# Cosine attention and a GELU layer on one core: score passes split by heads and laid beside the values passes

## The chip, the core and the metric

The kernel runs on one core of one Trainium2 chip. The metric is the time of one execution in microseconds (us). Before the change three runs took 401.39, 401.69 and 401.60 us, a median of 401.6 us. The engines are named as in the profile: PE (TensorE matmuls), PEld (its weight loads), DVE (VectorE), ACT (ScalarE), POOL (GpSimd), SP (SyncE, which issues most DMAs).

## What is computed

```python
q, k, v: (8 batches, 12 heads, 448 rows, 64)          # float32, as is everything below
q_n = q / (norm(q) + 1e-6);  k_n = k / (norm(k) + 1e-6)
p   = softmax(q_n @ k_n.T / tau)                       # tau = 0.1
x   = (p @ v), heads side by side: (3584, 768)
out = gelu(x @ moe_w_in) @ moe_w_out                   # 768 -> 2048 -> 768
```

## The kernel before, in words

**Units of work.** The 12 heads of a batch are three groups of four heads (`NQ = 3`, 24 groups in all). A group's rows are cut into `C = 7` chunks of 64 keys. The order of every instruction is written out by hand, and each engine executes its own list strictly in the order in which the code issues to it.

**A score pass** is `scores` (L232-244) for one chunk: four 64x64 matmuls that cover the four quarters of the array, two with rows 0-63 and two with rows 64-127. It fills a pair of PSUM banks, and one ACT instruction (`exps`, L252) turns the pair into `pt` in bf16. There are three such pairs, numbered 0, 1 and 2; `visit(1, 2)` (L647) makes the next two score passes into pairs 1 and 2.

**A values pass** is one chunk of `values` (L317): again four 64x64 matmuls, two with the array's rows 0-63 and two with rows 64-127, that accumulate `o` over the seven chunks in a pair of banks. `weighted` (L371) makes the seven passes and lets DVE multiply `o` by the inverse sums into `x` (`normalise`, L362).

**Stages.** For batch b the program runs `attention(b)` and then `first(b)`. `first(b)` is the layer 768 -> 2048 (`hp`, L462, 96 matmuls of 448 columns, GELU on ACT, L887). The second layer (`op`, L399, 384 columns) of the batch before is cut into single matmuls in the list `fill`, and `attention(b)` spends them between stretches of attention with `run()`: the tuple `parts` says how many each `run()` takes. There are 96 of them in the odd batches and 128 in the even ones. I number them from 1. A piece is 16 of them, accumulated in one PSUM bank and copied out by DVE (L403). Two banks, called mm0 and mm1 in `mm_tile` (L102), serve the pieces alternately, so piece n can start only when DVE has copied piece n-2. The `hp` blocks of `first` use the same two banks besides the three pairs; the table `pairs` in `first` says which block of two goes to which pair.

**Sums of the softmax.** From batch 2 on the sums are not made by PE. POOL adds up the seven chunks of one group during `attention(b)` and of another during `first(b)` (`folded`, L263); DVE adds up the third itself in `first(b)` (`gathered`, L265-270, seven instructions). DVE then turns each total into inverse sums in `turned_all` (L276, L278, L281) and `inverted_all` (L290, L294), and lays them out in `spread` (L357). `turned_all` starts with two transposes (`ta`, L276) that read what POOL has added up.

**Norms.** For later groups ACT squares (L158), DVE reduces (L168), ACT makes a logarithm and an exponential (L175, L180), DVE the inverse (`se` L186, `rn` L188), and POOL scales q and k (`scale`, L204). The scaled q and k are transposed by DMA.

**Before, attention from batch 3 on** visits seven stretches, with a `run()` ahead of each: visits 1, 2, seven values passes, visit 1; visits 2, 1, 0; visits 2, 0, values, visit 2; three times visits 0, 2, 1; visits 1, 2, values, visit 1. That is 21 score passes and 21 values passes a batch. Score passes run ahead: those of batch b's stage belong to the third group of batch b and the first two of batch b+1. In batch 7 only seven are left, and visits beyond them do nothing.

Of the kernel before, what the change touches and what calls it, by code (L numbers as in the profile page):

```python
# [10 lines left out]
BF16 = mybir.dt.bfloat16  # L11
# [5 lines left out]
def kernel(  # L17
# [280 lines left out]
    def sums(g, chunks=range(C)):  # L298
        for c in chunks:
            if c == 0:  # L300
                bank_t[g, "sm"] = ps_acc.tile([128, 512], F32, tag="sm", name=f"sm{g}") if g < NQ else \
                    mm_tile(f"sm{g}", aside=0)
            for s in range(2):
                if g < NQ:
                    nc.tensor.matmul(bank_t[g, "sm"][64 * s:64 * (s + 1), :S],  # L305
                                     lhsT=ones2.rearrange("p a h r -> p (a h r)"), rhs=pt_t[g, s, c],
                                     start=(c == 0), stop=(c == C - 1), tile_position=(0, 64 * s))
                    continue

                half = 2  # L310
                for i in range(2) if c == half else ((c - (c > half)) % 2,):
                    r = 32 * (2 * s + i)
                    cols = slice(i * S // 2, (i + 1) * S // 2) if c == half else slice(0, S)
                    nc.tensor.matmul(bank_t[g, "sm"][r:r + 32, cols], lhsT=ones, rhs=pt_t[g, s, c][:, cols],  # L314
                                     start=(c < 2), stop=(c >= C - 2), tile_position=(0, r))

    def values(g, chunks=range(C), p=None):  # L317
        for c in chunks:
# [328 lines left out]
    def visit(*pairs):  # L647
        for p in pairs:
            g, c = divmod(at[0], C)
            at[0] += 1  # L650
            if g < NG:
                scores(g, ((0, c), (1, c)), p)
                exps(g, ((0, c), (1, c)))

    def attention(b, fill):
        fill = list(fill)
        if b == 1:
            parts = iter((20, 13, 14, 17, 16, 16))
        elif b == 2:
            parts = iter((22, 12, 12, 13, 11, 13, 11, 11, 11, 6, 6))  # L660
        elif len(fill) == 128:
            parts = iter((20, 18, 18, 18, 18, 18, 9, 9))
        else:
            parts = iter((14, 13, 14, 14, 14, 13, 7, 7))

        def run(n=None):
            for _ in range(next(parts) if n is None else n):
                fill.pop(0)()

        def norms(n):  # L670
            if n < len(groups):
                logs(n)
                roots(n)
                done[root] = n + 1

        def inverted_norms(n):
            if n < len(groups):
                inverses(n)

        def squared(n, i):  # L680
            if n < NU:
                square(n, ((nc.scalar, i),))
                done[square] = n + 1

        def reduced(n, i):
            if n < NU:
                reduce(n, i)
                done[reduce] = n + 1

        x_t[b] = xp.tile([128, KD, S], BF16, tag="x", name=f"x{b}")  # L690
        g0, u = b * NQ, b * NQ + 1
        run()
        if b == 1:
            upto(scale, u + 3)
            upto(load_v, b + 2)
            upto(transposes, u + 3)
            upto(load_qk, g0 + NQ + 2)
            upto(square, u + 4)
            visit(0, 1, 2)
            run()  # L700
            visit(0, 1, 2)
            run()
            upto(load_qk, g0 + NQ + 3)
            visit(0, 1)
            upto(square, u + 5)
            run()
            visit(0, 1, 2)
            both(g0, 0)
            upto(load_v, b + 3)
            upto(load_qk, g0 + NQ + 4)  # L710
            visit(1, 2)
            upto(reduce, u + 4)
            run()
            visit(1, 2, 0)
            both(g0 + 1, 1)
            visit(2, 0)
            logs(6)
            roots(6)
            run()
            both(g0 + 2, 2)  # L720
            inverses(6)
            done[root] = 7
        elif b == 2:
            upto(scale, u + 3)
            upto(load_qk, g0 + 6)
            upto(transposes, u + 3)
            upto(scale, u + 4)
            upto(load_qk, g0 + 7)
            upto(transposes, u + 4)
            visit(0, 1, 2)  # L730
            run()
            visit(0, 1, 2)
            norms(9)
            inverted_norms(9)
            upto(scale, u + 5)
            upto(transposes, u + 5)
            upto(load_qk, g0 + 9)
            upto(square, u + 6)
            run()
            visit(1, 2)  # L740
            total(g0)
            weighted(g0, 0)
            visit(1, 2)
            squared(u + 6, 0)
            run()
            visit(1, 2, 0)
            run()
            reduced(u + 5, 0)
            visit(1, 2)
            squared(u + 6, 1)  # L750
            total(g0 + 1)
            weighted(g0 + 1, 0)
            visit(1, 2)
            reduced(u + 5, 1)
            folded(g0 + 2, range(C - 1))
            run()
            for i in range(2):
                reduced(u + 6, i)
            visit(1, 2, 0)
            folded(g0 + 2, range(C - 1, C))  # L760
            upto(load_v, b + 3)
            run()
            visit(1, 2, 0)
            run()
            visit(1, 2, 0)
            run()
            visit(1, 2, 0)
            norms(10)
            run()
            turned_all(g0 + 2)  # L770
            run()
            inverted_norms(10)
            inverted_all(g0 + 2)
            visit(1, 2)
            weighted(g0 + 2, 0)
            visit(1)
        else:
            upto(scale, u + 5)
            upto(transposes, u + 5)
            upto(load_qk, g0 + 9)  # L780
            visit(1, 2)
            weighted(g0, 0)
            visit(1)
            reduced(u + 5, 0)
            squared(u + 6, 0)
            folded(g0 + 2, range(3))
            run()
            reduced(u + 5, 1)
            visit(2, 1, 0)
            folded(g0 + 2, range(3, 6))  # L790
            run()
            reduced(u + 6, 0)
            for h in range(2):
                spread(g0 + 1, h)
            visit(2, 0)
            weighted(g0 + 1, 1)
            visit(2)
            squared(u + 6, 1)
            folded(g0 + 2, range(6, 7))
            upto(load_v, b + 3)  # L800
            run()
            visit(0, 2, 1)
            run()
            reduced(u + 6, 1)
            visit(0, 2, 1)
            norms(2 * b + 6)
            turned_all(g0 + 2)
            run()
            inverted_norms(2 * b + 6)
            inverted_all(g0 + 2)  # L810
            visit(0, 2, 1)
            run()
            run()
            for h in range(2):
                spread(g0 + 2, h)
            visit(1, 2)
            weighted(g0 + 2, 0)
            visit(1)
        assert not fill, len(fill)

    def first(b):
# [3 lines left out]
        nc.scalar.preload_act_table_set(GELU_SET)  # L825
        u = (b + 1) * NQ + 1
        hps = dict(early) if b == 0 else {}
        pairs = ({0: 1, 2: 0, 6: 1, 8: 0}, {2: 0, 4: 1, 6: 2, 8: 0}, {2: 2, 4: 1, 8: 2})[min(b, 2)]
        ahead = 6 if b else 5

        def mm(m, kds):
# [12 lines left out]
        if b == 0:  # L844
            upto(square, u + 3)
            upto(scale, u + 1)
            upto(transposes, u + 1)
            upto(load_wo, 4)
            upto(reduce, u + 3)
        elif b == 1:  # L850
            upto(scale, u + 1)
            upto(transposes, u + 1)
            upto(load_qk, (b + 1) * NQ + 5)
            upto(square, u + 3)
            upto(reduce, u + 2)
        elif b + 1 < B:
            for n in range(3, 5):
                upto(scale, u + n)
                upto(transposes, u + n)
                upto(load_qk, (b + 1) * NQ + 4 + n)  # L860
            folded((b + 1) * NQ + 1)
            if u + 4 < NU:
                square(u + 4, ((nc.scalar, 0), (nc.scalar, 1)))
            if u + 5 < NU:
                square(u + 5, ((nc.scalar, 0),))
            upto(reduce, u + 5)
            gathered((b + 1) * NQ, 0)
            turned_all((b + 1) * NQ)
            inverted_all((b + 1) * NQ)
            spread((b + 1) * NQ, 0)  # L870
            spread((b + 1) * NQ, 1)
            turned_all((b + 1) * NQ + 1)
            inverted_all((b + 1) * NQ + 1)
            done[square] = u + 6
# [94 lines left out]
```

## Time and profile before

| what | value |
|---|---|
| median of three runs | 401.6 us |
| the profiled execution's own time | 401.45 us |
| its span, first to last instruction | 399.6 us |
| PE busy | 393.0 us (98%) |
| ACT, DVE, POOL busy | 266.9, 262.0, 250.6 us |
| `st` L242, 672 matmuls / `o` L328, 672 matmuls | 49.5 / 36.9 us |
| `op` L399, 864 matmuls / `hp` L462, 768 matmuls | 148.9 / 147.0 us |

The span leaves out 1.85 us of the execution's own time. Times below that look like 203.28 are microseconds from the start of the span. In the timeline view, a row gives start, length, engine, line, tile written and read, and how many instructions were merged; matmuls overlap, so the start of the next row, not the length, says when PE went on. In brackets stands the idle time of the engine before the row and what ended it. The stages of the profiled execution begin as follows: `attention(3)` at 151.57, `first(3)` at 176.72, `attention(4)` at 194.89, `first(4)` at 225.24, `attention(5)` at 243.41, `first(5)` at 268.56, `first(6)` at 317.07, `first(7)` at 357.05.

### The profile page before, as it was taken

The numbers are of one execution on the slowest core, as the hardware profiler recorded it, in microseconds if no ns is written. First come the engines' busy times: TensorE is split into PE (matmuls) and PEld (weight loads), VectorE is DVE, ScalarE is ACT, GpSimd is POOL, SyncE is SP. The second block draws the span as 40 slices with busy tenths as digits, with TensorE's granted clock in tenths as the row PEclk, the third lists the DMA queues.
The fourth block names the chain that finished last, engine by engine and source line by source line (L and its number), as shares of the span: only waits on it lengthen the run. The fifth ranks groups of instructions, "written<-read, shape, count | busy, mean of one in ns | idle before, by whom it ended". The sixth has DMA issues, their size and how long they took to land.

```text
span 399.6 us, 8019 instructions
## 1 busy us (share of the span) xinstructions
PE 393.0 (98%) x3245; PEld 205.6 (51%) x3245; DVE 262.0 (66%) x530; ACT 266.9 (67%) x386; POOL 250.6 (63%) x162
## 2 busy tenths in 40 slices
PE   7999999999999999999999999999999999999996
PEld 3444555555545555555555555555555555555564
DVE  5787214955487999679976599679975695470021
ACT  6995787557998877797576867788656746504300
POOL 5898804269699694969495981969677760910000
PEclk9999999999999999999999999999999999999999
DMA  8999999847296890679066770665032700130033
GB/s 289 260 258 216 203 220 303 176 105 222 52 263 221 160 227 2 181 126 275 21 116 153 174 204 0 178 111 133 2 85 52 171 14 2 41 79 2 0 81 80
DMA packets 66485, 54.52 MB, mean 136 GB/s; under 512 B 38672, under 2 KB 62352, under 8 KB 66448
## 3 DMA queue, kind: packets, MB, share of 16 engines
q1 hardware_dynamic: 54464, 41.79, 39.5%
q0 software_dynamic: 11600, 11.80, 18.7%
q8 instruction: 25, 0.41, 0.4%
q10 hardware_dynamic: 384, 0.43, 0.4%
q14 instruction: 12, 0.10, 0.1%
HBM read 45.61 MB, written 11.01 MB: 142 GB/s over the span
## 4 chain that ended last, share of the span: by engine, by line
PE 95%; DMA 2%; SPq 1%; DVE 1%; ACT 1%; issue 0%; ACTq 0%
PE hp L462 37%; PE op L399 36%; PE st L242 10%; PE o L328 8%; DMA qk<-in_k_dram 2%; PE op L418 1%; PE sm L305 1%; PE sm L314 1%; PE tp L221 1%; SPq L133 1%; ACT sq L158 0%; PE spin L456 0%; ACT pt L252 0%; DVE tr L336 0%; DVE rs L357 0%
## 5 line engine op out<-in xcount | busy, mean ns | idle before, releaser
L252 ACT ACTIVATE pt<-st 128x896 bf16<-128x896 f32 x168 | 143.1, 916 | 37.0 <-PE st L242 36.5
L399 PE MATMUL op<-wo,g 128*128 128x384 bf16 x864 | 148.9, 327 | 0.0
L462 PE MATMUL hp<-x,wi 128*128 128x448 bf16 x768 | 147.0, 353 | 0.1
L204 POOL TENSOR_TENSOR qkb<-qk,rn 128x896 bf16<-128x896 f32 (+1 forms) x50 | 80.3, 1628 | 62.5 <-DVE rn L188 61.1
L399 PEld LDWEIGHTS <-g 128*128 128x128 bf16 x864 | 81.0, 98 | 64.7 <-issue 14.1
L462 PEld LDWEIGHTS <-wi 128*128 128x128 bf16 x768 | 74.4, 98 | 71.5 <-issue 3.1
L887 ACT ACTIVATE g<-hp 128x448 bf16<-128x448 f32 x128 | 63.6, 552 | 66.9 <-PE hp L462 66.7
L263 POOL TENSOR_TENSOR acc<-acc,pt 128x896 f32<-128x896 f32 x55 | 103.8, 1886 | 4.3
L403 DVE COPY ot<-op 128x384 f32<-128x384 f32 x54 | 29.6, 548 | 78.1 <-PE op L399 75.7
L168 DVE TENSOR_REDUCE nq<-sq 128x14 f32<-128x896 f32 (+1 forms) x50 | 50.9, 1038 | 12.8 <-POOL sq L160 6.7
L242 PE MATMUL st<-qkT 64*64 64x448 bf16 x672 | 49.5, 358 | 0.2 <-ACT pt L252 0.2
L160 POOL TENSOR_TENSOR sq<-qk 128x896 f32<-128x896 f32 x18 | 29.9, 1683 | 16.3 <-DMA qk<-in_q_dram 11.9
L328 PE MATMUL o<-pt,v 64*64 64x448 bf16 x672 | 36.9, 350 | 0.3 <-DVE x L362 0.3
L270 DVE TENSOR_TENSOR acc<-acc,pt 128x896 f32<-128x896 f32 x30 | 33.0, 1099 | 1.0
L362 DVE TENSOR_TENSOR x<-o,rs 128x448 bf16<-128x448 f32 x48 | 27.5, 608 | 9.1 <-PE o L328 8.8
L158 ACT ACTIVATE sq<-qk 128x896 f32<-128x896 f32 (+1 forms) x32 | 27.8, 899 | 2.4 <-DMA qk<-in_q_dram 1.9
L242 PEld LDWEIGHTS <-qkT 64*64 64x64 bf16 x672 | 16.7, 105 | 24.4 <-issue 18.2
L263 POOL TENSOR_TENSOR acc<-pt 128x896 f32<-128x896 bf16 x11 | 20.7, 1879 | 13.2 <-ACT pt L252 13.2
L357 DVE STREAM_TRANSPOSE rs<-rc 128x448 f32<-128x448 f32 x48 | 28.1, 621 | 0.4
L328 PEld LDWEIGHTS <-v 64*64 64x64 bf16 x672 | 19.1, 107 | 13.9 <-issue 3.1
L276 DVE STREAM_TRANSPOSE ta<-acc 128x448 f32<-128x448 f32 x32 | 18.6, 618 | 5.9 <-POOL acc L263 5.7
L278 DVE TENSOR_REDUCE sa<-ta 128x28 f32<-128x896 f32 x16 | 17.4, 1087 | 0.6
(49 smaller groups left out, 163.0 us busy)
## 6 DMA issues: line engine op xcount, KB each, us to landing
qk<-in_q_dram SPq DMA_DIRECT2D x23, 448.0 KB, 4.9
qk<-in_k_dram SPq DMA_DIRECT2D x23, 448.0 KB, 5.7
out_dram<-ot SPq DMA_DIRECT2D x48, 192.0 KB, 3.0
v<-in_v_dram POOLq DMA_DIRECT2D x7, 672.0 KB, 7.1
wo<-in_moe_w_out_dram POOLq DMA_DIRECT2D x4, 768.0 KB, 12.1
wi<-in_moe_w_in_dram POOLq DMA_DIRECT2D x4, 512.0 KB, 14.4
out_dram<-ot SPq DMA_DIRECT2D x12, 96.0 KB, 2.2
wi<-in_moe_w_in_dram POOLq DMA_DIRECT2D x4, 256.0 KB, 14.9
```

Of the source, the lines that this page charges most:

```text
L160: eng.tensor_tensor(sq, t, t, ALU.mult)
L168: nc.vector.tensor_reduce(nq_t[n][:, j, i], sq_t[g, i][:, s0:s1], mybir.AxisListType.X, ALU.add)
L204: eng.tensor_tensor(qkb[:, i, :, s0:s1].rearrange("p c s d -> p s c d"), t[:, i, s0:s1], rn[:, i].to_broadcast([128, s1 - s0, C, D]), ALU. ...
L242: nc.tensor.matmul(st[cols, n, :S], lhsT=qkT[rows, 1, c, cols], rhs=qkT[rows, 0, :, cols], start=True, stop=True, tile_position=(64 * s, 6 ...
L252: nc.scalar.activation(pt, st[:, :, :S], AF.Exp, scale=inv_tau)
L263: nc.gpsimd.tensor_tensor(acc_t[g], all_t[g][:, 0] if c == 1 else acc_t[g], all_t[g][:, c], ALU.add)
L270: nc.vector.tensor_tensor(acc_t[g], acc_t[g], all_t[g][:, c], ALU.add)
L328: nc.tensor.matmul(bank_t[g, h][cols, :S], lhsT=v_t[g][rows, s, c, :], rhs=pt_t[g, s, c][rows], start=(c == 0), stop=(c == C - 1), tile_po ...
L399: nc.tensor.matmul(ps[:, :NH], lhsT=g_t[sb][:, kf, t * 128:(t + 1) * 128], rhs=wo[:, kf, ni * NH:(ni + 1) * NH], start=(kf == 0), stop=(kf ...
L403: nc.vector.tensor_copy(ot[:, ni * NH:(ni + 1) * NH], ps[:, :NH])
L462: nc.tensor.matmul(t, lhsT=wi[:, kd, m * 128:(m + 1) * 128], rhs=x_t[b][:, kd, :], start=(kd == 0), stop=(kd == KD - 1))
L887: nc.scalar.activation(g_t[sb][:, m, hf * S:(hf + 1) * S], hps.pop(m), AF.Gelu)
```

## The change

From batch 3 on, three of the seven stretches get a fourth score pass, and one stretch of three goes. The added pass is not made at once: the new `half_score` makes two of its four matmuls, those of rows 0-63, next to the two matmuls of the first values chunk that use rows 64-127; the values of the two row halves then go on one chunk apart (`value`), and the two other score matmuls, of rows 64-127, are made next to the last values matmuls of rows 0-63. Each half goes into one of the two banks of the `op` pieces and not into a pair, and has an exponential of its own of 128x448 (`half_exp`). With `aside=0`, `mm_tile` hands out the bank that the next piece will use and does not change the turn. `mixed` issues all that, with one whole score pass inside the values (`amid`) and two behind them (`behind`).

The new order of a batch is: mixed with 1 inside and 2, 1 behind; visits 2, 0, 1; mixed with 0 inside and 1, 0 behind; visits 1, 2, 0 twice; mixed with 2 inside and 0, 2 behind. `o` lies in pairs 0, 2 and 1. Score and values passes are as many as before. In batch 7 the first mixed stretch has four score passes, the second has three with whole passes, and the last has values alone.

The numbers of matmuls in `parts` change, `spread` of the second group moves ahead of the second stretch, the sums that DVE makes in `first` use pair 1, and the `hp` blocks from batch 3 on use pairs 0, 2, 0.

```diff
+    def value(g, c, h):
+        rows = slice(64 * h, 64 * (h + 1))
+        for s in range(2):
+            nc.tensor.matmul(bank_t[g, h][64 * s:64 * (s + 1), :S], lhsT=v_t[g][rows, s, c, :],
+                             rhs=pt_t[g, s, c][rows], start=(c == 0), stop=(c == C - 1),
+                             tile_position=(64 * h, 64 * s))
...
+    def half_score(g, c, s, last):
+        qkT, rows = qkT_t[g], slice(64 * s, 64 * (s + 1))
+        st = mm_tile(f"sh{g}_{c}_{s}", aside=None if last else 0)
+        for h in range(2):
+            cols = slice(64 * h, 64 * (h + 1))
+            nc.tensor.matmul(st[cols, :S], lhsT=qkT[rows, 1, c, cols], rhs=qkT[rows, 0, :, cols],
+                             start=True, stop=True, tile_position=(64 * s, 64 * h))
+        return st
+
+    def half_exp(g, c, s, st):
+        pt_t[g, s, c] = all_t[g][:, c, s]
+        nc.scalar.activation(pt_t[g, s, c], st[:, :S], AF.Exp, scale=inv_tau)
+
+    def mixed(g, p, amid, behind, last=False):
+        q, c = divmod(at[0], C)
+        if q >= NG:
+            weighted(g, p)
+            return
+        at[0] += 1
+        if q not in all_t:
+            all_t[q] = ptp.tile([128, C, 2, S], BF16, tag="pt", name=f"pt{q}")
+        o = pair(p, f"o{g}")
+        bank_t[g, 0], bank_t[g, 1] = o[:, 0], o[:, 1]
+        st = half_score(q, c, 0, False)
+        value(g, 0, 1)
+        half_exp(q, c, 0, st)
+        for k in range(C - 1):
+            value(g, k, 0)
+            value(g, k + 1, 1)
+            if k == 0:
+                visit(*amid)
+        value(g, C - 1, 0)
+        st = half_score(q, c, 1, last)
+        half_exp(q, c, 1, st)
+        visit(*behind)
+        for h in range(2):
+            if (g, h) not in rs_t:
+                spread(g, h)
+            normalise(g, h)
...
         elif len(fill) == 128:
-            parts = iter((20, 18, 18, 18, 18, 18, 9, 9))
+            parts = iter((22, 20, 16, 26, 25, 10, 9))
         else:
-            parts = iter((14, 13, 14, 14, 14, 13, 7, 7))
+            parts = iter((14, 17, 13, 18, 17, 9, 8))
...
-            visit(1, 2)
-            weighted(g0, 0)
-            visit(1)
+            mixed(g0, 0, (1,), (2, 1))
             reduced(u + 5, 0)
             squared(u + 6, 0)
             folded(g0 + 2, range(3))
             run()
             reduced(u + 5, 1)
-            visit(2, 1, 0)
-            folded(g0 + 2, range(3, 6))
-            run()
-            reduced(u + 6, 0)
             for h in range(2):
                 spread(g0 + 1, h)
-            visit(2, 0)
-            weighted(g0 + 1, 1)
-            visit(2)
+            if b + 1 < B:
+                visit(2, 0, 1)
+            else:
+                visit(2, 0)
+                weighted(g0 + 1, 1)
+                visit(2)
+            folded(g0 + 2, range(3, 6))
+            run()
+            reduced(u + 6, 0)
+            if b + 1 < B:
+                mixed(g0 + 1, 2, (0,), (1, 0))
             squared(u + 6, 1)
             folded(g0 + 2, range(6, 7))
             upto(load_v, b + 3)
             run()
-            visit(0, 2, 1)
-            run()
             reduced(u + 6, 1)
-            visit(0, 2, 1)
+            visit(1, 2, 0)
             norms(2 * b + 6)
             turned_all(g0 + 2)
             run()
             inverted_norms(2 * b + 6)
             inverted_all(g0 + 2)
-            visit(0, 2, 1)
-            run()
+            visit(1, 2, 0)
             run()
             for h in range(2):
                 spread(g0 + 2, h)
-            visit(1, 2)
-            weighted(g0 + 2, 0)
-            visit(1)
+            run()
+            mixed(g0 + 2, 1, (2,), (0, 2), True)
...
-        pairs = (..., {2: 2, 4: 1, 8: 2})[min(b, 2)]
+        pairs = (..., {2: 2, 4: 1, 8: 2}, {2: 0, 4: 2, 8: 0})[min(b, 3)]
...
-            gathered((b + 1) * NQ, 0)
+            gathered((b + 1) * NQ, 0 if b < 3 else 1)
```

## The prediction

> **What bounds the kernel now.** I read the chain of work that ended last first, then PE's waits. The first line is the chain's share by engine; the others read: waiting engine, who released it, total us, times, longest.
>
> ```profile
> PE 95%; DMA 2%; SPq 1%; DVE 1%; ACT 1%; issue 0%; ACTq 0%
> ```
> ```profile
> PE spin L456 <- DVE root L92: 1.9, 1, 1.9
> PE tp L221 <- POOL qkb L204: 0.6, 1, 0.6
> PE o L328 <- DVE x L362: 0.3, 1, 0.3
> PE st L242 <- ACT pt L252: 0.2, 1, 0.2
> ```
>
> PE never waits after the first batch, so only two things can change the time: fewer PE slots, or a new wait on PE. Next I read PE's timeline of batch 3 (columns: start, length, engine, line, tiles, form, count).
>
> ```profile
> 151.57 2.44 PE L399 MATMUL op<-wo,g 128*128 128x384 bf16 x14
> 153.94 0.57 PE L242 MATMUL st<-qkT 64*64 64x448 bf16 x8
> 154.34 1.49 PE L328 MATMUL o<-pt,v 64*64 64x448 bf16 x28
> 155.67 0.36 PE L242 MATMUL st<-qkT 64*64 64x448 bf16 x4
> 155.96 2.29 PE L399 MATMUL op<-wo,g 128*128 128x384 bf16 x13
> 158.17 0.76 PE L242 MATMUL st<-qkT 64*64 64x448 bf16 x12
> 158.87 2.45 PE L399 MATMUL op<-wo,g 128*128 128x384 bf16 x14
> ```
>
> Starts, not lengths, give the pace. Ten passes take 155.96-153.94 = 2.02, three take 0.70, so a pass is 1.32/7 = 0.189, and entering and leaving a stretch adds 0.70-0.567 = 0.13. In batch 7 a block of 55 op matmuls takes 9.04 (346.56 to 355.60); 14 take 2.37 above, so one is 6.67/41 = 0.163 and a block adds 0.09. One stretch fewer saves 0.13+0.09 = **0.22 us**.
>
> **The saving.** The 32 matmuls of a mixed block (28 values, four halves) are eight passes, as 7+1 were. Score passes today go in the same order over the array's quarters as the new passes will (both columns of one row half, then of the other), so I take 0.189 for them; at worst the halves follow one another, 0.38. A mixed stretch is 11 passes, 2.21. Batches 3 to 6 lose one stretch each, batch 7 one of four: 5 x 0.22 = 1.1 us saved.
>
> **ACT.** A half exponential is bounded by the GELU row of the same shape (552 ns, next start 0.44 later) and the whole one (916 ns, 0.81): I take 0.44 spacing. Two halves cost 0.07 more than one whole. ACT has slack, so this is free inside a stage. At the stage's end it is not: two passes now follow the values, not one. From the start of the last stretch, half 2 is made at 1.54; its exponential starts 0.41 later (pass 224.95, exponential 225.36), 1.95; the last two at 2.39 and 3.20. `first` begins at 2.21. Its fifth matmul, due 0.77 later, needs pair 0, free at 2.39+0.91+0.05 (PE followed its one ACT release by 0.05) = 3.35: a wait of **0.38**, in batches 3 to 6, 1.5 in all. ACT's table load, 1.05 after `first` begins today (226.29-225.24), comes at 4.14-2.21 = 1.93, so what ACT feeds in `first`, the squares that DVE's backlog waits for, slips 0.88.
>
> **Where the moved work meets DVE's queue: piece 5.** `parts` is now 14, 17, 13, 18, so `turned_all` is issued after matmul 62; before it was after 69. Piece 3 ends at 64. Its copy (L403) thus stands in DVE's list behind the transposes `ta`, which wait for POOL. Piece 5 (matmul 81) needs that bank. DVE and POOL in batch 3 now:
>
> ```profile
> 168.01 0.56 DVE L403 COPY ot<-op 128x384 f32<-128x384 f32 x1 [2.84 <-PE op L399]
> ...
> 171.84 1.17 DVE L276 STREAM_TRANSPOSE ta<-acc 128x448 f32<-128x448 f32 x2 [2.27 <-POOL acc L263]
> ...
> 174.93 0.56 DVE L403 COPY ot<-op 128x384 f32<-128x384 f32 x1
> ```
> ```profile
> 156.79 3.34 POOL L204 TENSOR_TENSOR qkb<-qk,rn 128x896 bf16<-128x896 f32 x2 [5.32 <-DVE rn L188]
> 160.09 1.88 POOL L263 TENSOR_TENSOR acc<-pt 128x896 f32<-128x896 bf16 x1
> 162.05 9.75 POOL L263 TENSOR_TENSOR acc<-acc,pt 128x896 f32<-128x896 f32 x5
> ```
>
> The copy at 168.01 is piece 3's, that at 174.93 piece 4's, which delays nothing today. POOL works without a gap from 156.79, released by DVE's `rn`, to 171.80; earlier scores cannot advance it. So piece 3's copy takes the place at 174.93 and PE may go on at 174.93+0.56+0.05 = 175.54. PE would be there at 153.94 +2.21 +2.86 (17 op) +0.70 +2.21 (13) +2.21 +3.02 (18) +0.70 +2.86 (17) +0.70 +0.17 (matmul 80) = 171.58. **Wait: 3.96.** Then 16 op (2.69) and 2.21: `first(3)` at 180.44, not 176.72: **+3.72**. Piece 4's copy is then past (177.71), before the last half needs its bank (178.23).
>
> **The first stretch of batches 4 and 6.** It comes after 22 matmuls. The first half needs the bank of piece 0, done at 16, whose copy is behind DVE's backlog from `first`:
>
> ```profile
> 199.61 0.33 DVE L188 RECIPROCAL rn<-se 128x28 f32<-128x28 f32 x1
> 199.86 0.49 DVE L403 COPY ot<-op 128x384 f32<-128x384 f32 x1
> 200.27 1.14 DVE L362 TENSOR_TENSOR x<-o,rs 128x448 bf16<-128x448 f32 x2
> ```
>
> Today nobody needs that copy before matmul 33. It ends 200.35-176.72 = 23.63 after `first` began; with the slip and the release, 24.56. PE arrives at 18.17 (`first`) +0.38 +3.67 (22 op) = 22.22. **Wait: 2.34.** From there to the stage's end PE takes today's 27.01 less two op (0.33) and a stretch (0.22), 26.46. Period 51.02, not 48.52: **+2.50** in each.
>
> In batches 3, 5 and 7 the stretch comes after 14, inside piece 0, and the other bank is free.
>
> **Batch 5.** From the start of `first(4)`: first stretch at 18.17+0.38+2.37 = 20.92. The third stretch waits some 0.2 for piece 1's copy (backlog, slipped). The copy behind `ta` ends now at 266.69+0.56, 42.01 after `first(4)` began; slipped and released, 42.94. PE is due at 20.92+17.64+0.2 = 38.76. **Wait: 4.18.** The period is 42.94+2.69+2.21 = 47.84, not 43.32: **+4.52**.
>
> **Batch 7.** No squares hold DVE here. POOL's fold starts once both halves of chunk 0 are through ACT, 2.63 after the first stretch; it takes 11.71 as now (339.96 to 351.67); `ta` to the copy's end 3.66 as now (351.71 to 355.37): release at 18.08. Matmul 81 is due at 2.21+2.86+2.02+7.98 = 15.07. **Wait: 3.0**. Then 2.69 and seven values passes (1.45): 22.22. With 20.92 ahead, 43.14, not 39.98: **+3.16**.
>
> **Sum.** 3.72+2.50+4.52+2.50+3.16 = 16.4. By cause: 16.0 of waits and 1.5 at the stage ends, less 1.1. On the profiled execution's own time, 401.45, that is 417.85; the median lies 0.15 higher, so I say **418.0**.
>
> **The clock.** The profile shows clock 1.000 and, after the start, no PE gap over 0.6. At the start, after 1.9 idle, nine spin matmuls take 3.46 (0.37 apart); later ones take 0.19. If a stall brought that back, it would cost about 8 x 0.18 = 1.5 each; I bound it by 0 and 1.5 for each of the five, 7 in all, and take 0 since no row shows a slow matmul after a short gap.
> [...]
>
> **Rivals.**
> - *Likeliest*, 418: chance 0.75.
> - *The stretches' saving alone*: 401.45-1.1 = 400.3, or 401.9 with the waits at the stage ends. It needs POOL's folds to end four microseconds sooner, and DVE's backlog 2.3 sooner. From a wait of 0.2 a batch on, the saving is gone. POOL's gapless row speaks against it. 0.05.
> - *DVE's backlog is shorter*, so that batches 4 and 6 do not wait, and piece 5 does: 418-4.7 = 413.3. For it: the slip is my own working. Against it: the copy is late by 1.4 even without slip. 0.07.
> - *The clock falls* after two to five of the stalls, 1.5 each: 421 to 425. The slow spins speak for it, the shortness of the stalls against it. 0.10.
> - *The split doesn't overlap*: the halves of a mixed pass follow one another, 13 stretches x 8 x 0.19 = 20 more, some of it inside the waits: 425 to 438. 0.03.
>
> **How the numbers follow.** A measurement of this kernel tells about 0.2% (0.8 us) from no change. Faster comes only from the second case: 0.03; its other half is the same: 0.02; slower 0.95. The range 412.5 to 422.5 takes in the first and third case and the lower half of the fourth.
>
> **What would show it.** In the profile after: `op` waiting for DVE three times (3 to 4.2 us, batches 3, 5, 7), the halves waiting for DVE's copy twice by 2.3, `hp` waiting for ACT four times by 0.4, and mixed passes 0.189 apart. I am wrong if DVE's copy of piece 3 comes ahead of `ta`, if POOL's folds end earlier, or if mixed passes are 0.38 apart.

## The result, and the profile after

Before: median 401.64 us (401.39 to 401.75, four runs). After: **426.76 us** (423.64 to 427.7, four runs). The ratio is 1.061 (95% interval 1.056 to 1.067): slower, by 25.1 us where I had said 16.4, and above the range. In the experiments below four executions, two of the kernel before and two of **mended**, were disturbed (6 to 11 us longer, clock 0.98) and are left out of the ratios.

The page after, the first line of the chain of work and the row of the granted clock (forty slices, tenths of full speed):

```profile
PE 67%; DVE 12%; POOL 9%; issue 5%; ACT 4%; DMA 2%; SPq 1%; POOLq 1%; ACTq 0%
...
PEclk9999999999999999799899999969989999999999
```

The chain was PE alone; now DVE and POOL carry 21% of it. And the clock, 9 in every slice before, falls in four places; the mean of the profiled run is 0.975. PE's waits after (waiting, releaser: total us, times, longest):

```profile
PE op L406 <- DVE ot L410: 10.6, 3, 4.0
PE sh L667 <- DVE ot L410: 4.5, 2, 2.3
...
PE hp L469 <- ACT pt L252: 1.0, 4, 0.2
```

These are the three, two and four waits that were forecast. In DVE's timeline of batch 3 the copy of piece 3, the last row, stands behind the transposes `ta`, which waited for POOL; PE's timeline beside it shows who waited for that copy. (The whole trace lies 1.2 us later than that of before at this point: batch 3 began at 152.78 and not at 151.57. A wait of 0.81 us in the first batch, which none of the other traces has, makes up most of it.)

```profile
173.06 1.17 DVE L276 STREAM_TRANSPOSE ta<-acc 128x448 f32<-128x448 f32 x2 [3.81 <-POOL acc L263]
...
176.15 0.56 DVE L410 COPY ot<-op 128x384 f32<-128x384 f32 x1
```
```profile
172.65 0.34 PE L406 MATMUL op<-wo,g 128*128 128x384 bf16 x1
176.76 5.28 PE L406 MATMUL op<-wo,g 128*128 128x384 bf16 x16 [3.77 <-DVE ot L410]
181.97 0.58 PE L667 MATMUL sh<-qkT 64*64 64x448 bf16 x2
...
184.46 0.93 PE L469 MATMUL hp<-x,wi 128*128 128x448 bf16 x4
185.63 17.56 PE L469 MATMUL hp<-x,wi 128*128 128x448 bf16 x92 [0.24 <-ACT pt L252]
```

Take starts again. From matmul 80 to 81 it is 176.76-172.65 = 4.11, less 0.17: a wait of 3.94, forecast 3.96. But the 16 matmuls behind it take 5.21 where sixteen take 2.69. PE works and is slow. The table by windows of this kernel says why (stretch: its length; busy us and count for PE, PEld, DVE, ACT, POOL; granted clock; DMA):

```profile
172.35:175.76 3.41, 0.63 (x9) 0.11 (x2) 2.61 (x6) 2.53 (x3) 1.50 (x2) 1.00 0.34 25
175.77:182.59 6.82, 5.83 (x24) 2.60 (x27) 4.56 (x14) 0.00 (x0) 4.96 (x4) 0.50 0.71 148
182.60:186.00 3.40, 3.16 (x46) 1.54 (x39) 1.19 (x3) 3.16 (x5) 3.40 (x3) 1.00 0.65 157
```

While PE waited, its clock went from 1.00 to 0.50 (at 175.76) and stayed there for 6.8 us.

### The profile page after: what moved, and what is told of

Its sections match the earlier page's. It is cut to its first block, busy times and chain, and to the rows that moved or that the text cites. A ratio compares the mean times of both kernels' runs of the same rounds, so it can differ in the third digit from the quotient of the medians.

```text
span 425.9 us, 8029 instructions
## 1 busy us (share of the span) xinstructions
PE 401.6 (94%) x3245; PEld 211.4 (50%) x3245; DVE 262.4 (62%) x530; ACT 268.0 (63%) x399; POOL 250.7 (59%) x162
## 4 chain that ended last, share of the span: by engine, by line
PE 67%; DVE 12%; POOL 9%; issue 5%; ACT 4%; DMA 2%; SPq 1%; POOLq 1%; ACTq 0%
PE op L406 26%; PE hp L469 23%; POOL acc L263 8%; PE st L242 6%; PE o L320 4%; DVE acc L270 3%; PE o L335 3%; DMA qk<-in_k_dram 2%; DVE ta L276 2%; ACT pt L252 2%; DVE sa L278 2%; PE op L425 1%; DVE sa L281 1%; PE sm L305 1%; DVE nq L168 1%
## 5 line engine op out<-in xcount | busy, mean ns | idle before, releaser
L406 PE MATMUL op<-wo,g 128*128 128x384 bf16 x864 | 153.8, 334 | 10.6 <-DVE ot L410 10.6
L252 ACT ACTIVATE pt<-st 128x896 bf16<-128x896 f32 x155 | 132.5, 916 | 25.8 <-PE st L242 25.2
L406 PEld LDWEIGHTS <-g 128*128 128x128 bf16 x864 | 82.9, 100 | 77.8 <-issue 28.5
L242 PE MATMUL st<-qkT 64*64 64x448 bf16 x620 | 47.2, 363 | 0.3 <-ACT pt L252 0.3
L673 ACT ACTIVATE pt<-sh 128x448 bf16<-128x448 f32 x26 | 14.1, 544 | 33.7 <-PE sh L667 33.2
L242 PEld LDWEIGHTS <-qkT 64*64 64x64 bf16 x620 | 18.4, 107 | 20.8 <-issue 13.2
L320 PE MATMUL o<-pt,v 64*64 64x448 bf16 x364 | 26.7, 378 | 0.0
L335 PE MATMUL o<-pt,v 64*64 64x448 bf16 x308 | 17.5, 351 | 0.5 <-DVE x L369 0.5
```

The source lines that it names most:

```text
L242: nc.tensor.matmul(st[cols, n, :S], lhsT=qkT[rows, 1, c, cols], rhs=qkT[rows, 0, :, cols], start=True, stop=True, tile_position=(64 * s, 6 ...
L252: nc.scalar.activation(pt, st[:, :, :S], AF.Exp, scale=inv_tau)
L320: nc.tensor.matmul(bank_t[g, h][64 * s:64 * (s + 1), :S], lhsT=v_t[g][rows, s, c, :], rhs=pt_t[g, s, c][rows], start=(c == 0), stop=(c == ...
L335: nc.tensor.matmul(bank_t[g, h][cols, :S], lhsT=v_t[g][rows, s, c, :], rhs=pt_t[g, s, c][rows], start=(c == 0), stop=(c == C - 1), tile_po ...
L406: nc.tensor.matmul(ps[:, :NH], lhsT=g_t[sb][:, kf, t * 128:(t + 1) * 128], rhs=wo[:, kf, ni * NH:(ni + 1) * NH], start=(kf == 0), stop=(kf ...
```

## Experiments

The kernel before, run again beside the first four kernels below, had a median of 401.94 us, and beside the last three 401.92; each ratio is to these executions. The first two kernels each take away one of the two kinds of wait.

**first_run_16**: two halves less to wait for.

```diff
-            parts = iter((22, 20, 16, 26, 25, 10, 9))
+            parts = iter((16, 22, 20, 26, 25, 10, 9))
```

> Theory (the halves of the first stretch of batches 4 and 6 wait 2.27 us each for DVE's copy of piece 0, and the clock falls behind each wait): with 16 matmuls ahead of that stretch the first half takes the other bank, both waits go, and with them two stretches at half clock of about 1.7 each: 426.8 - 4.5 - 3.4 = 419, mean clock about 0.984 against 0.975 to 0.983. Rival (DVE's backlog only moves the wait to matmul 33, which needs the same copy): the waits stay under another line and the time stays at 424 to 428.

Measured 418.67 us (417.13 to 419.63), ratio 1.042 (1.041 to 1.044); the profiled run has clock 0.991. The two waits of `sh` are gone. In their place matmul 17 waits twice for the exponential of the second half, 0.3 each, since the half now sits in the bank that piece 1 wants at once:

```profile
PE op L406 <- DVE ot L410: 10.5, 3, 3.9
...
PE op L406 <- ACT pt L673: 0.6, 2, 0.3
```

The first theory holds. The wait did not move to matmul 33. The mean clock, 0.983 to 0.991 over the four executions, was mostly above the 0.984 that I expected: in the profiled run the half clock behind the waits of batches 3 and 5 lasted for 3.4 us each and not for 6.8.

**late_totals**: in odd batches `turned_all` behind the `run()` that ends with matmul 88, so behind the copies of pieces 3 and 4.

```diff
             norms(2 * b + 6)
-            turned_all(g0 + 2)
+            if b % 2 == 0:
+                turned_all(g0 + 2)
             run()
             inverted_norms(2 * b + 6)
-            inverted_all(g0 + 2)
+            if b % 2 == 0:
+                inverted_all(g0 + 2)
             visit(1, 2, 0)
             run()
+            if b % 2:
+                turned_all(g0 + 2)
+                run()
+                inverted_all(g0 + 2)
             for h in range(2):
                 spread(g0 + 2, h)
-            run()
+            if b % 2 == 0:
+                run()
```

> Theory (piece 5 waits for the copy of piece 3, which stands behind the transposes ta that wait for POOL): with ta issued after the copies of pieces 3 and 4 in the odd batches the three waits (3.77, 3.97, 2.85) go, and the half clock behind two of them (2.8 and 2.4): 426.8 - 10.6 - 5.2 = 411. The two waits of batches 4 and 6 stay. Rival (the inverse sums now come too late): the first layer waits for x instead, over 1 us in each of batches 3, 5 and 7, and the time stays over 414.

Measured 407.09 us (406.78 to 408.9), ratio 1.014 (1.012 to 1.016). The three waits of `op` are gone, and `first` waits for no `x`, so the rival falls. The time is 4 us lower than I expected, 3.3 of it because I had counted a fall of the clock behind each of the two waits that stay (1.64 and 1.69). In the profiled run (408.9) only one of them has it. These are the stretches around the two, each wait 2.27 us idle:

```profile
198.28:201.69 3.41, 1.14 (x11) 0.61 (x13) 2.91 (x13) 0.00 (x0) 0.60 (x1) 1.00 0.00 0
201.70:205.10 3.40, 3.40 (x44) 2.15 (x36) 0.19 (x1) 1.60 (x3) 2.73 (x2) 0.50 0.00 0
293.85:297.26 3.41, 1.77 (x11) 0.97 (x10) 3.14 (x13) 0.62 (x3) 0.00 (x0) 1.00 0.00 0
297.27:300.67 3.40, 2.78 (x48) 1.89 (x48) 1.42 (x4) 2.17 (x4) 3.17 (x2) 1.00 0.00 0
```

The first wait lies inside the 3.41 us ahead of 201.70, which hold 1.14 us of PE's work, and the 3.40 us behind read 0.50. The second (295.6 to 297.89) lies across 297.27, which is 28 times 3.413 us after 201.70 (the last section says where that length comes from): the 3.41 us ahead hold 1.77 us of work, and the clock reads 1.00 on both sides. The other three executions (406.78 to 407.23) are shorter by 1.7 to 2.1 us and have a mean clock of 0.999, so neither wait seems to have lowered it there; their traces were not kept.

**both_waits_gone**: both edits.

> Both edits in one. Theory (the change is a saving of 1.1 us of changeovers, 1.0 us of waits of the first layer for ACT, 0.2 in batch 5, and the rest is the five waits and the clock): 401.6 - 1.1 + 1.2 = 401.7, clock 1.000, mixed passes 0.189 apart. Rival (the mixed passes or the half exponentials themselves cost time): over 404 with no wait of PE for DVE over 0.5 us.

Measured 403.29 us (nine executions, eight of them 402.78 to 403.94; the ninth, 408.69 at clock 0.996, is in the ratio, and its trace was not kept), ratio 1.0047 (1.0017 to 1.0078), clock 1.000 in the profiled run. Past the first batch PE waits in no row of the waits view for DVE, and the clock holds:

```profile
PE hp L469 <- ACT pt L252: 1.0, 4, 0.2
PE op L406 <- ACT pt L673: 0.6, 2, 0.3
```

The two causes, the five waits and the clock behind them, account for all but 1.4 us of the loss. My sum was too low by 1.6. I had added PE's waits in `hp` as the waits view gives them (0.24 of idle time each, counted from modelled ends), and had left out the two new ones of matmul 17. By starts the four waits of `hp` are 0.40 each (four matmuls take 1.17 from 184.46 to 185.63 above, not 0.77) and those of matmul 17 are 0.36 each: -1.1+1.6+0.7+0.2 = +1.4 on 401.45, and the profiled run took 402.78.

**spins_in_waits**: the changed kernel with its waits filled, to tell the wait from the clock. The added work's output is read by nobody.

```diff
+    def keep(n, p):
+        st = pair(p, "keep")
+        for _ in range(n):
+            nc.tensor.matmul(st[:, 0, :S], lhsT=ident, rhs=wo[:, 0, :S], start=True, stop=True)
...
-            parts = iter((14, 17, 13, 18, 17, 9, 8))
+            parts = iter((14, 17, 13, 18, 17, 1, 8, 8))
...
+            if b % 2 == 0:
+                keep(11, 2)
             mixed(g0, 0, (1,), (2, 1))
...
             visit(1, 2, 0)
             run()
+            if b % 2:
+                keep(14 if b == 7 else 20, 0 if b == 7 else 1)
+                run()
```

> The changed kernel with idle matmuls into a bank that nobody reads, 20 or 14 ahead of piece 5 in the odd batches and 11 ahead of the first half in batches 4 and 6, so that PE works while it would wait. Theory (PE's idleness lowers the clock): clock 1.000, no slow matmul after the waits, though nothing comes earlier: 426.8 - 8.5 = 418.3, which is what the waits alone were forecast to make. Rival (the slow matmuls after a wait come from what the other engines do then): the matmuls after the waits stay at 0.33 apart and the time stays at 424 to 428.

Measured 418.94 us (418.56 to 419.26), ratio 1.042 (1.041 to 1.044), clock 0.999. **Work that does nothing makes the changed kernel 8 us faster**, and executions that spread over 4 us now lie within 0.7. PE in batch 3 with the spins:

```profile
171.63 0.34 PE L406 MATMUL op<-wo,g 128*128 128x384 bf16 x1
172.40 3.94 PE L468 MATMUL keep<-wo,ident 128*128 128x448 bf16 x20 [0.43 <-ACT pt L252]
176.18 2.76 PE L406 MATMUL op<-wo,g 128*128 128x384 bf16 x16
178.87 0.38 PE L672 MATMUL sh<-qkT 64*64 64x448 bf16 x2
```

Piece 5 comes no earlier than in the changed kernel (24.42 us after the start of `attention(3)`, where it was 23.98), but its 16 matmuls take 2.69 (178.87-176.18) again. So the slow matmuls came from PE's idleness and not from what the other engines do there, whose work is the same in both kernels. With the clock held, the time is the forecast 418.0 and 0.9 more; 0.7 of that is piece 5 coming later, by 0.44 in batch 3 and 0.24 in batch 5.

**wait_shortened** and **wait_shorter_still**: late_totals with shorter waits in batches 4 and 6.

```diff
-            parts = iter((22, 20, 16, 26, 25, 10, 9))
+            parts = iter((27, 15, 16, 26, 25, 10, 9))
```

and `(31, 11, 16, 26, 25, 10, 9)`.

> The kernel late_totals with 27 matmuls, not 22, ahead of the first stretch of batches 4 and 6, which leaves of the two waits 2.34 - 5 x 0.163 = 1.53 us each. Without a fall of the clock: 401.5 - 1.1 + 1.6 + 0.2 + 3.1 = 405.3, clock 1.000. [...] Theory two (1.5 us are enough): 405.3 to 408.7, spread over steps of about 1.7, some at clock 0.992 to 0.996.

> The same with 31 matmuls ahead: two waits of 0.88 us each. Without a fall of the clock 404.0. Theory one (about 2 us are needed) and theory two (1.5 us are enough) both say 404.0 in all executions, clock 1.000; a third (any gap lowers it) says up to 407.4.

Measured 405.22 us (four executions, 405.07 to 405.29), ratio 1.008 (1.007 to 1.010); by starts the two waits are 1.5 each, as worked out. This is the first:

```profile
195.15 4.55 PE L406 MATMUL op<-wo,g 128*128 128x384 bf16 x27
201.15 0.38 PE L667 MATMUL sh<-qkT 64*64 64x448 bf16 x2 [1.46 <-DVE ot L410]
```

None of the eight waits lowered the clock: the mean clocks of 0.998 to 1.000 leave no room for it, since one stretch of 3.4 us at half clock, the shortest in the traces after and of first_run_16 and late_totals, takes 0.004 off the mean (3.41 x 0.5 / 403). So 1.5 us were not enough in any of the eight: theory one holds here, and theory two falls. With the shorter waits 404.68 us (404.27 to 406.04, and one of 409.19, which is in the ratio), ratio 1.009 (1.006 to 1.012): 0.7 above the sum. By starts 0.37 of that is the block of 11 `op` behind the first stretch of batches 4 and 6, which takes 2.07 and 2.06 us and not 1.88; its second matmul is number 33, which needs the bank of the second half, so a wait for that half's exponential is the likely reason, though the waits view does not list it. What the execution of 409.19 had (clock 0.991) stays open; its trace was not kept.

**mended**: what is left of the change without its waits. Beside the edit of late_totals:

```diff
-    def mixed(g, p, amid, behind, last=False):
+    def mixed(g, p, amid, behind, last=False, then=None):
...
         visit(*behind)
+        if then:
+            then()
         for h in range(2):
...
-            parts = iter((22, 20, 16, 26, 25, 10, 9))
+            parts = iter((14, 2, 22, 20, 26, 25, 10, 9))
...
-            parts = iter((14, 17, 13, 18, 17, 9, 8))
+            parts = iter((14, 2, 15, 13, 18, 17, 9, 8))
...
-            mixed(g0, 0, (1,), (2, 1))
+            mixed(g0, 0, (1,), (2, 1), then=run)
...
-            for h in range(2):
-                spread(g0 + 1, h)
...
-        for m in (0, 2, 3, 4, 5, 1) if b > 1 else range(ahead):
+        for m in (0, 2, 3, 4, 5, 1) if b == 2 else range(ahead):
```

> The change with what was found mended: ta after the copies of pieces 3 and 4 in odd batches, 14 matmuls ahead of the first stretch in all batches and two more ahead of the normalisation (so that the copy of piece 0 is issued before it), the second group's spread left to the normalisation, and the blocks of the first layer in the order 0, 1, 2, 3, 4, 5, so that the fifth matmul needs no pair. Theory (nothing but the five saved changeovers is left): 401.6 - 1.1 = 400.5, ratio 0.997, clock 1.000, no wait of PE over 0.2 us after the first batch. Rival (the mixed stretches cost what the waits hid, or the wait moves to the ninth matmul of the first layer): 401.5 or more.

Measured 400.84 us over all twelve executions, 400.65 over the ten undisturbed ones (400.15 to 402.3), ratio **0.9969** (0.9953 to 0.9984): faster than before by 0.3%, about 1.2 us. The saving stands where the changeovers went: by starts `attention(3)` takes 24.92 where it took 25.15, and each of `attention(4)` to `attention(7)` is shorter by 0.22 or 0.23 too, 1.14 together, while `first(3)` and `first(4)` take 18.17 as before. PE's waits are those of the first batch alone, 1.9 and at most 0.3 us. The last stretch of batch 3:

```profile
174.18 0.38 PE L667 MATMUL sh<-qkT 64*64 64x448 bf16 x2
174.19 0.56 PE L320 MATMUL o<-pt,v 64*64 64x448 bf16 x6
...
175.91 0.55 PE L242 MATMUL st<-qkT 64*64 64x448 bf16 x8
176.39 3.96 PE L469 MATMUL hp<-x,wi 128*128 128x448 bf16 x20
```

Eleven passes from 174.18 to 176.39, 2.21 as forecast; the half passes cost what whole ones do.

## Why the prediction was wrong

**Right, in kind and size**, by starts in the trace after, with the forecast behind each: piece 5 waits 3.94 (3.96), 4.14 (4.18) and 3.01 (3.0) in batches 3, 5 and 7; the first half waits 2.34 (2.34) in batches 4 and 6; the third stretch of batch 5 0.2 (0.2); `hp` 0.40 (0.38) four times; a mixed stretch takes 2.21. first_run_16, late_totals and both_waits_gone took the waits away and with them the loss. The saving is there too, 1.14 by stage for the forecast 1.1, as mended shows.

**Wrong: the step on the clock.** The prediction bounded it "by 0 and 1.5 for each of the five, 7 in all, and take 0 since no row shows a slow matmul after a short gap". The trace before had no such gap at all past its start, so its silence said nothing. In the trace after, the clock fell to 0.50 behind the two longest waits, 3.94 and 4.14, and behind the two of 2.34 as well, and it stayed at 1.00 behind the one of 3.01. What the waits cost behind them, from PE's restart, by starts:

| wait | PE's work behind it | at full clock | lost |
|---|---|---|---|
| batch 3, 3.94 | 7.70 to the first `hp` | 4.90 | 2.80 |
| batch 4, 2.34 | 7.20 through the stretch and 20 `op` | 5.56 | 1.64 |
| batch 5, 4.14 | 7.30 to the first `hp` | 4.90 | 2.40 |
| batch 6, 2.34 | 7.25 as in batch 4 | 5.56 | 1.69 |
| batch 7, 3.01 | 2.69 to the last values | 2.69 | 0 |

Together 8.5, where the prediction had 0. With the forecast's 16.4 that is 24.9 on 401.6, or 426.5; 426.76 was measured, and spins_in_waits, with the clock held, gives 418.94. So the missing term is the clock, and it is shown by taking it away, not only by the sum. Its chance, 0.10, was far too low, and the price per fall too: 1.64 to 2.80, not 1.5.

## What to carry to other kernels

A wait on TensorE may not be paid once: behind four of the five waits of the changed kernel (2.34 to 4.14 us) the granted clock was 0.50 for 3.4 or 6.8 us. In these traces a stall of 2.3 us or more cost itself and, behind it, either nothing or some 1.6 to 2.8 us, so price it with that range, or fill it with matmuls that nobody reads (418.94 us for 426.76 here). When work is moved along a list that several engines share, look at what is issued between the old place and the new on the *other* engines: here seven matmuls' difference in a tuple (62 for 69) put a copy behind an instruction that waits for POOL. Count what PE loses by starts; idle times from modelled ends were short by 0.07 to 0.17 (0.24 for 0.40 in `hp`, 3.77 for 3.94 at piece 5).

## What I had not expected of the hardware

In the trace after, the stretches at half clock behind four of the five waits begin at 175.76, 209.90, 278.16 and 312.30, which lie 10, 20 and 10 times 3.413 us apart, and last 6.8, 3.4, 6.8 and 3.4 us. So I cut that trace into steps of 3.413 us, counted from these starts. I call the steps windows; they are a way to cut a trace. These are the window ahead of each fall but the first (shown above), and the two that hold the wait of batch 7:

```profile
206.48:209.89 3.41, 1.14 (x22) 0.76 (x24) 2.33 (x11) 0.37 (x1) 1.23 (x1) 1.00 0.00 0
...
274.75:278.16 3.41, 1.36 (x16) 0.38 (x15) 1.75 (x3) 2.78 (x4) 2.42 (x2) 1.00 0.08 5
...
308.88:312.29 3.41, 1.14 (x13) 0.67 (x15) 2.79 (x13) 0.00 (x0) 0.72 (x1) 1.00 0.00 0
...
373.74:377.15 3.41, 2.54 (x16) 1.41 (x15) 1.71 (x3) 0.00 (x0) 1.63 (x1) 1.00 0.00 0
377.15:380.56 3.41, 1.44 (x9) 0.87 (x9) 3.18 (x13) 0.00 (x0) 0.00 (x0) 1.00 0.12 25
```

In the windows ahead of the four falls PE was busy for 0.63, 1.14, 1.36 and 1.14 us. The wait of batch 7, longer (3.01) than those of batches 4 and 6 (2.34), lies across 377.15: its two windows hold 2.54 and 1.44 us of work, the clock reads 1.00 in both, and the 16 matmuls behind the wait took 2.69. In late_totals 1.14 us of work stood ahead of a fall, and 1.77 ahead of none. The trace of first_run_16, cut in the same steps from its own falls, has the three waits of piece 5, in batches 3, 5 and 7:

```profile
172.13:175.54 3.41, 0.07 (x1) 0.07 (x1) 3.24 (x9) 1.59 (x2) 0.42 (x1) 1.00 0.69 88
175.55:178.96 3.41, 3.41 (x12) 1.59 (x12) 3.05 (x10) 0.00 (x0) 2.62 (x2) 0.50 1.06 229
178.97:182.38 3.41, 3.41 (x52) 1.85 (x51) 1.17 (x3) 1.92 (x4) 3.41 (x3) 1.00 0.22 46
...
271.11:274.52 3.41, 0.53 (x4) 0.33 (x4) 3.20 (x9) 0.94 (x2) 0.00 (x0) 1.00 0.85 113
274.53:277.94 3.41, 3.41 (x13) 1.58 (x12) 2.62 (x9) 0.00 (x0) 3.08 (x2) 0.50 0.87 205
...
366.69:370.10 3.41, 1.48 (x10) 0.89 (x10) 3.18 (x13) 0.00 (x0) 0.00 (x0) 1.00 0.13 28
```

There 0.07 and 0.53 us stood ahead of a fall and 1.48 ahead of none: the run's mean clock of 0.991 has room for two stretches of 3.4 us in 415.4 (0.992) and for no third (0.988). So of these eleven windows in three traces, the seven in which PE was busy for 1.36 us or less, as the profile models it, were followed by half clock, and the four with 1.44 or more were not. What holds in other kernels these runs do not show.

How long the half clock lasted differs too. In the trace after, the window from 175.76, in which PE worked from 176.76 on, was followed by a second one at half clock; in first_run_16 PE worked through the whole window from 175.55, and the next was at full clock. So the same wait for piece 5 in batch 3 cost 2.80 us behind it in the one trace and 1.7 in the other (its 16 matmuls took 4.37 there and not 2.69). In these three traces the falls do not keep to the start of the program: the first behind a wait comes a whole number of steps of 3.413 us and 1.7 us after the start of the span in the trace after, 1.5 in first_run_16 and 0.3 in late_totals. I take that for one cause of the spread of 423.6 to 427.7 us, an estimate from these three traces: two executions had a mean clock of 0.975, two of 0.983. It is not the only one, since the two with 0.983 lie 2.5 us apart.

One more thing about the reading of 1.000 in the kernel before: the view says 1.00 also for 1.95 to 5.21 us, where nine spin matmuls start 0.37 apart and not 0.19. At the start of that trace the pace of the matmuls tells more than this column does.
